# Centring the first two tiles ahead of their projections, with finer weight transfers and a shorter warm-up, in a linear-attention and gated-MLP kernel

## The chip, the cores and the metric

The kernel runs on one core of one Trainium2 chip. The metric is the device time of one execution in microseconds (us); the number quoted for a kernel is the median of its runs. The kernel before takes 193.78 us (three runs, 193.72 to 194.22). Every run also reports the mean clock that TensorE was granted (1.0 is full speed); runs with a low clock and a time over 1.5% above the fastest are called slow, and are compared with nothing here.

Engines: PE is TensorE (matmuls; PEld is its weight load), DVE is VectorE, ACT is ScalarE, POOL is GpSimd, SP is SyncE, which only issues DMA transfers. An ending q (SPq) means the engine's queue of issues.

## The reference, cut

```python
x = A_x                                                  # 2048 rows of 448, bf16
h  = x + attn(_layernorm(x), wqkv, wo)                   # linear attention, 16 heads of 28
h2 = h + (gelu(n(h) @ w_gate) * (n(h) @ w_up)) @ w_down  # n = _layernorm; 448 -> 1792 -> 448

# inside attn, with q, k, v = split(x @ wqkv):
phi = lambda t: where(t > 0, t + 1, exp(t)) + 1e-6
kv  = einsum(phi(k), v);  z = sum(phi(k))                # sums over all 2048 rows
o   = phi(q) @ kv / (phi(q) . z + 1e-6)
```

The layernorm has no learned scale. A row's `(x - mean) * rstd` can therefore be multiplied with the weights first and by `rstd` afterwards, since `rstd` is one number per row. The change uses this.

## The kernel before

The 2048 rows are 16 tiles of 128. Every operation is a task in a graph; a table `ORDERS` says in which order each of the five engines runs its tasks, and the orders have been tuned. Each engine works through its list strictly in order and waits on semaphores.

For each tile: statistics on DVE, `ln` and `rstd` on ACT (two tiny instructions, about 0.2 to 0.3 us each), then the normalised tile is transposed so that it can be projected. Tiles 0 to 3 are transposed by PE, tiles 4 to 15 by DMA.

```python
def ln_tile(t):
    ln_stats(t, ...)                       # DVE
    ln_rstd_act(t, ...)                    # ACT: Ln, then Exp(-0.5 * ln)
    if t < 4:                              # tiles 0..3
        op("dve", tensor_scalar(xnn, x_sb, mean, rstd, subtract, mult), name="normD_t")
        ...                                # 4 PE transposes of xnn; copies out of PSUM on ACT and DVE
    else:                                  # tiles 4..15
        ln_negm(t, ...)                    # POOL
        op("pool", tensor_scalar(xnn, x_sb, -mean, rstd, add, mult), name="normP_t")
        G.add("sp", dma_start_transpose(xnT[t], xnn), name="xT_t")
...
def k_tile(t):                             # K projection, 4 matmuls of 448 columns
    G.add("pe", proj(...), name="k_t")
    act_exp(activation(e1, psK, Exp), name="ek_t")
    op("dve", tensor_scalar(e1, e1, 1+EPS, 0, min, max), name="ck_t")
    op("dve", scalar_tensor_tensor(pk, psK, EPS, e1, max, add), name="pk_t")
    ...                                    # then matmuls of pk with xnn, accumulated over all tiles
def q_tile(t):                             # Q projection
    ...                                    # ACT: Exp "eq_t" and Relu "rq_t", both out of PSUM
```

(Python shortened; cuts are marked by dots.) The projections share four PSUM slots, and a slot comes free when ACT (and for K also DVE) has read it. Before the first transposes PE runs 40 dummy matmuls of 128 columns (`WARM = 40`), because its clock starts at half speed (in the profile of before they start 107 ns apart at first, and 56 ns apart once the clock has opened).

The order in which the first transfers are issued on SP: x tile 0, the Q/K weights in one piece of 672 KB and a tail of 112 KB, x tiles 2 and 3 together, 4 to 7, 8 to 11, 12 to 15, then the V and output weights. (x tile 1 is issued by ACT.)

## Time and profile before

| | before |
|---|---|
| time, median of three runs | 193.78 us |
| span of the profiled execution | 197.8 us, a slow one: clock 0.95 |
| PE busy | 193.7 us, 98% |
| share of PE in the chain that ended last | 90% |
| first projection starts | 6.31 us |

The page of the kernel before, its head, the busy times (share of the span, number of instructions), and the chain of waits by engine:

```profile
span 197.8 us, 4145 instructions
...
PE 193.7 (98%) x1572; PEld 106.9 (54%) x1572; DVE 132.0 (67%) x355; ACT 78.1 (39%) x226; POOL 50.7 (26%) x92
...
PE 90%; DMA 4%; DVE 4%; POOL 1%; issue 0%; DVEq 0%; POOLq 0%
```

PE is nearly always busy and holds nine tenths of the chain. So the reading was: what can be won is what PE does not do in its first microseconds. PE's timeline of that stretch (columns: start, duration, engine, line, operation, result and inputs, shapes, count; in brackets the idle time just before, and what ended it):

```profile
1.11 4.30 PE L342 MATMUL ps<-ones_bf 128*128 128x128 bf16 x40 [1.11 <-POOL ones_bf L315]
5.37 0.38 PE L378 MATMUL ps<-ident,xnn 128*128 128x128 bf16 x4
6.07 0.40 PE L378 MATMUL ps<-ident,xnn 128*128 128x128 bf16 x4 [0.32 <-DVE xnn L370]
6.31 3.30 PE L404 MATMUL ps<-wqk_sb,xnT 128*128 128x448 bf16 x16
```

The reader sees 40 warm-up matmuls from 1.11 us, the transposes of tile 0 at 5.37, those of tile 1 at 6.07 after a wait of 0.32 us for DVE, and then sixteen projection matmuls. Up to 6.31 us PE does, apart from these transposes, no work that counts.

### The profile page before, as it was taken

How to read it: one execution, taken by the hardware profiler on the slowest of the kernel's cores; microseconds unless marked ns; L12 is line 12 of the kernel's file. 1: busy time of each engine (PE TensorE's matmuls, PEld its weight loads, DVE VectorE, ACT ScalarE, POOL GpSimd, SP SyncE). 2: the span in 40 equal slices, each digit the busy share in tenths (PEclk: the TensorE clock that was granted, in tenths of full speed). 3: DMA queues.
4: the chain of work that ended last, by engine and by line, in shares of the span. 5: the costliest groups of instructions: out<-in, count | busy, mean ns of one | idle time of the engine just before them, and what ended most of it. 6: DMA issues, size and time to landing. Idle time of an engine off the chain costs nothing.

```text
span 197.8 us, 4145 instructions
## 1 busy us (share of the span) xinstructions
PE 193.7 (98%) x1572; PEld 106.9 (54%) x1572; DVE 132.0 (67%) x355; ACT 78.1 (39%) x226; POOL 50.7 (26%) x92
## 2 busy tenths in 40 slices
PE   7999999999999999999999999999999999999995
PEld 7554555555767776654454445444444454444454
DVE  3899988999999989988786537244445422444412
ACT  3797645599943324141330420023444200334200
POOL 7067710640451955235222024000000000000000
PEclk9999999999999999999999999999999999999999
DMA  6966449994587046420217272600200010100011
GB/s 194 375 174 88 94 96 209 221 215 63 102 291 124 16 50 117 102 53 23 56 26 153 57 56 52 133 21 30 46 0 3 0 46 4 46 0 3 0 46 46
DMA packets 35331, 16.97 MB, mean 86 GB/s; under 512 B 27696, under 2 KB 34032, under 8 KB 35312
## 3 DMA queue, kind: packets, MB, share of 16 engines
q1 hardware_dynamic: 35168, 16.60, 38.4%
q8 instruction: 12, 0.20, 0.4%
q10 hardware_dynamic: 144, 0.11, 0.2%
q14 instruction: 7, 0.06, 0.1%
HBM read 8.26 MB, written 1.84 MB: 51 GB/s over the span
## 4 chain that ended last, share of the span: by engine, by line
PE 90%; DMA 4%; DVE 4%; POOL 1%; issue 0%; DVEq 0%; POOLq 0%
PE ps L603 42%; PE ps L575 22%; PE ps L404 9%; PE ps L523 7%; PE ps L423 5%; PE ps L605 3%; DMA x_sb<-in_A_x_dram 2%; DVE st L348 2%; DMA xnT<-xnn 2%; DVE pk L417 1%; PE ps L471 0%; PE ps L462 0%; POOL wqk_sb L302 0%; PE ps L550 0%; DVE xnn L370 0%; DVE mv L349 0%
## 5 line engine op out<-in xcount | busy, mean ns | idle before, releaser
L605 PE MATMUL ps<-hnT,wgu_sb 64*128 64x512 bf16 (+1 forms) x490 | 89.9, 342 | 0.0
L603 PE MATMUL ps<-hnT,wgu_sb 64*128 64x512 bf16 (+1 forms) x490 | 89.6, 342 | 0.0
L623 ACT ACTIVATE gl<-ps 128x256 bf16<-128x256 f32 x112 | 37.1, 381 | 88.5 <-PE ps L605 86.4
L603 PEld LDWEIGHTS ps<-hnT,wgu_sb 64*128 64x128 bf16 x490 | 46.3, 96 | 35.1 <-issue 3.1
L625 DVE TENSOR_TENSOR hh<-ps,gl 128x256 bf16<-128x256 f32 x112 | 42.5, 416 | 34.0 <-ACT gl L623 33.7
L605 PEld LDWEIGHTS ps<-hnT,wgu_sb 64*128 64x128 bf16 x490 | 45.2, 96 | 3.7 <-DVE hh L625 0.5
L575 PE MATMUL ps<-wd_sb,hh 128*128 128x448 bf16 (+1 forms) x238 | 45.2, 351 | 0.0
L575 PEld LDWEIGHTS ps<-wd_sb,hh 128*128 128x128 bf16 x238 | 23.3, 99 | 21.1 <-issue 1.3
L404 PE MATMUL ps<-wqk_sb,xnT 128*128 128x448 bf16 x128 | 28.2, 362 | 0.1
L488 POOL TENSOR_TENSOR t<-pq,zbc 128x448 f32<-128x448 bf16 x15 | 16.6, 1115 | 33.3 <-DVE pq L484 20.5
L579 DVE TENSOR_TENSOR x_sb<-ps,x_sb 128x448 bf16<-128x448 f32 (+1 forms) x17 | 10.0, 592 | 19.6 <-PE ps L575 19.6
L348 DVE BATCH_NORM_STATS2 st<-x_sb 128x6 f32<-128x448 bf16 x32 | 19.1, 612 | 3.5 <-DMA x_sb<-in_A_x_dram 3.4
L404 PEld LDWEIGHTS ps<-wqk_sb,xnT 128*128 128x128 bf16 x128 | 12.3, 99 | 12.1 <-DMA xnT<-xnn 0.5
L423 PE MATMUL ps<-pk,xnn 128*128 128x448 bf16 x64 | 14.4, 363 | 0.0
L523 PE MATMUL ps<-w,pqnT 112*128 112x448 bf16 x64 | 14.1, 362 | 0.0
L558 POOL TENSOR_SCALAR hn<-x_sb,nm,rs 128x448 bf16<-128x448 bf16 x14 | 10.9, 779 | 8.1 <-DMA hnT<-hn 7.4
L529 DVE TENSOR_TENSOR x_sb<-ps,x_sb 128x448 bf16<-128x448 f32 x16 | 9.5, 617 | 3.8 <-PE ps L523 3.8
L415 ACT ACTIVATE e<-ps 128x448 bf16<-128x448 f32 x16 | 8.7, 541 | 5.4 <-PE ps L404 3.6
L417 DVE SCALAR_TENSOR_TENSOR pk<-ps,e 128x448 bf16<-128x448 f32 x16 | 9.9, 616 | 0.2
L388 POOL TENSOR_SCALAR xnn<-x_sb,nm,rs 128x448 bf16<-128x448 bf16 x12 | 9.0, 749 | 3.5 <-ACT rs L357 3.5
L423 PEld LDWEIGHTS ps<-pk,xnn 128*128 128x128 bf16 x64 | 6.5, 101 | 6.2
L495 DVE TENSOR_TENSOR pqn<-pq,rd 128x448 bf16<-128x448 bf16 x16 | 9.6, 622 | 0.0
(65 smaller groups left out, 125.0 us busy)
## 6 DMA issues: line engine op xcount, KB each, us to landing
out_dram<-x_sb SPq DMA_DIRECT2D x15, 112.0 KB, 1.7
wd_sb<-in_B_w_down_dram SPq DMA_DIRECT2D x1, 1568.0 KB, 7.7
x_sb<-in_A_x_dram SPq DMA_DIRECT2D x3, 448.0 KB, 5.4
wgu_sb<-in_B_w_gate_dram SPq DMA_DIRECT2D x1, 896.0 KB, 11.9
wgu_sb<-in_B_w_up_dram SPq DMA_DIRECT2D x1, 896.0 KB, 16.5
wqk_sb<-in_A_wqkv_dram SPq DMA_DIRECT2D x1, 672.0 KB, 4.8
wgu_sb<-in_B_w_gate_dram SPq DMA_DIRECT2D x1, 672.0 KB, 6.0
wgu_sb<-in_B_w_up_dram SPq DMA_DIRECT2D x1, 672.0 KB, 8.4
```

Of the source, the lines that this page charges most:

```text
L348: op("dve", lambda e: e.bn_stats(st[:, t, :], src_ap), [b_src], [b_st[t]], "bnst%s_%d" % (tag, t))
L404: ins = e.matmul(ps[:, bk, 0:D], xnT[:, t, k, :], wqk_sb[:, k, c0:c0 + D], start=(k == 0), stop=(k == 3))
L417: op("dve", lambda e: e.scalar_tensor_tensor(pk[:, ip, :], psK, EPS, e1[:, i, :], ALU.max, ALU.add), [b_ps[bk], b_e1[i]], [b_pk[ip]], "pk_ ...
L423: ins = e.matmul(ps[:, BK_PT[c], 0:D], xnn[:, t % XN_R, c * 128:(c + 1) * 128], pk[:, ip, :], start=(t == 0), stop=(t == T - 1))
L488: op(eng, lambda e, t=t, n=n: e.tensor_tensor(t1[:, n, :], pq[:, t, :], zbc[:, :], ALU.mult), [b_pq[t]] + b_z, [b_t1[n]], "t1%s_%d" % (eng ...
L523: ins = e.matmul(ps[:, BK_OUT[n], 0:D], pqnT[0:GW, i2, n, g, :], w2[:, g, :], start=(g == 0), stop=(g == NG - 1))
L558: op("pool", lambda e, t=t, sh=sh: e.tensor_scalar(hn[:, sh, 0:D], x_sb[:, t, :], nm2[:, t:t + 1], rs2[:, t:t + 1], ALU.add, ALU.mult), [b ...
L575: ins = e.matmul(psO, hh[:, j, (t % HR) * 128:(t % HR + 1) * 128], wd_sb[:, j, c0:c1], start=(j == 0), stop=(j == NJ - 1))
L603: e.matmul(psG[:, jj * N:(jj + 1) * N], wgu_sb[A_, k, j * 128:(j + 1) * 128], hnT[A_, ka_, c0:c0 + N], start=(k == 0), stop=(k == NK - 1))
L605: ins = e.matmul(psU[:, jj * N:(jj + 1) * N], wgu_sb[B_, k, j * 128:(j + 1) * 128], hnT[B_, kb_, c0:c0 + N], start=(k == 0), stop=(k == NK ...
L623: G.add("act", lambda e, gi=gi, cs_=cs_, psG=psG: e.activation(gl[:, gi, cs_], psG[:, cs_], AF.Gelu_apprx_tanh), r=[b_ps[BK_G[i]]], w=[b_g ...
L625: op("dve", lambda e, dst=dst, srcU=srcU, srcL=srcL: e.tensor_tensor(dst, srcU, srcL, ALU.mult), [b_ps[BK_U[i]], b_glh], [b_ar[j_][t % HR] ...
```

## The change

The intent is to start the first projection sooner and to keep it from waiting for the weights:

- Tiles 0 and 1 are only centred (`x - mean`) before they are transposed and projected. `rstd` is applied later, as the scale of the Exp and Relu with which ACT reads their projections. K's `max` on DVE becomes a Relu on ACT for these two tiles. The normalised tiles are still needed for the later matmuls with `pk`; POOL makes them.
- The Q/K weights come in four pieces, with x tile 2 between the second and the third; the following x transfers are smaller too.
- 32 warm-up matmuls in place of 40.
- The order table of every engine was computed anew.

```diff
@@ cut to its core; the order tables, all renumbered, are left out @@
+    CEN = (0, 1)
-    WARM = 40
+    WARM = 32
...
-        dma_w3("sp", wqk_sb, 0, 2 * D, b_wqk, "dwqk")
-        dma_w1("sp", wqk_sb, 0, 2 * D, b_wqk, "dwqk_t")
-        dma_x("sp", 2, 4)
-        dma_x("sp", 4, 8)
+        dma_wqk(0)
+        dma_wqk(1)
+        dma_x("sp", 2, 3)
+        dma_wqk(2)
+        dma_wqk(3)
+        dma_x("sp", 3, 4)
+        dma_x("sp", 4, 6)
+        dma_x("sp", 6, 8)
...
+                if t in CEN:
+                    op("dve", lambda e: e.tensor_scalar(xc[:, t % 2, 0:D], x_sb[:, t, :], mv1[:, t, 0:1], None, ALU.subtract), ..., "cen_%d" % t)
...
-            else:
+            if t >= N_PE_TR or t in CEN:
                 ln_negm(t, t + 1, mv1, nm1, b_mv1, b_nm1, "1")
                 op("pool", ..., "normP_%d" % t)
...
+            sc = rs1[:, t:t + 1] if t in CEN else 1.0
+            eks.append(act_exp(lambda e: e.activation(e1[:, i, :], psK, AF.Exp, scale=sc), ..., "ek_%d" % t))
+            if t in CEN:
+                act_exp(lambda e: e.activation(pk[:, ip, :], psK, AF.Relu, scale=sc), ..., "rk_%d" % t)
+                op("dve", ..tensor_scalar(e1, e1, 1.0, EPS, ALU.min, ALU.add).., "ck_%d" % t)
+                op("dve", ..tensor_tensor(pk, pk, e1, ALU.add).., "pka_%d" % t)
...
+            act_exp(lambda e: e.activation(eq[:, t, :], ps[:, bk, 0:D], AF.Exp, scale=sc), ..., "eq_%d" % t)
+            act_exp(lambda e: e.activation(pq[:, t, :], ps[:, bk, 0:D], AF.Relu, scale=sc), ..., "rq_%d" % t)
```

## The prediction

> **What bounds the kernel now.** TensorE. The busy table has PE at 193.7 of 197.8 us (98%), and the chain of waits gives it 90%. Taking single matmuls, from the first projection at 6.31 us to the end they follow at the rate of their columns (197 ns for 448 at the granted clock of 0.95), with gaps of only 2.6 us in all; the largest are 0.28 us (9.6 us, transposes of tile 3) and 0.22 us (18.1 us, a wait for a DMA transpose). The profiled execution was a slow one; the timed ones took 193.78. The change leaves the matmul work alone, so it wins only what it takes off the first 6.31 us and those gaps.
>
> **What gates 6.31 us (timeline, landings).** x tile 0 lands at 3.34; statistics to 4.21; ln and rstd on ACT to 4.77; scaled subtract to 5.22; transposes at 5.36. Tile 1's scaled subtract waits for its rstd until 5.61, its transposes run at 6.06, and PE takes them before the first projection: 6.31. The big Q/K weight piece landed at 6.03, its tail at 6.29. The 40 warm-up matmuls run 1.11 to 5.36: spaced 107 ns up to 5.03, then 56 ns.
>
> **What the change does.**
> - Removes ln+rstd (0.6 us with hand-overs) ahead of tile 0's transposes. But DVE is in order: statistics 0, centre 0, statistics 1 (0.8), half the copy of tile 0 (0.2), centre 1 (0.38), then tile 1's transposes, which still precede the first projection. Adding up from 3.37: centre 1 done near 5.85, first projection near 6.2, only 0.1 us earlier.
> - Four weight pieces: at the roughly 400 KB/us of the DMA slices they land near 4.9, 5.4, 6.2 and 6.4, x tile 2 near 5.8 instead of 6.74. Weights leave the path; tile 2's transposes move from 9.45 to about 7.9.
> - Adds two Relu evictions on ACT (0.43 us each at their spacing), a scale operand on eight activations, two normalisations on GpSimd (0.75 each). The Trainium skill ("ScalarE: Activation LUTs", What ACT_TABLE_LOAD costs) gives 93 ns for each per-partition pointer operand; before has none on these evictions, so its trace can't confirm it. ACT is busy 4.94 of 5 us from 10 to 15 us; its queue delays tile 2's copy out of PSUM: tile 2's K projection at 9.8 to 10.1, against 10.21.
> - Shorter warm-up: 32 x 107 ns ends near 4.55, before the transposes, which frees nothing. The skill ("TensorE: Matmul & The Clock Gate", Part 1) says the clock opens after a free-running activity window of about 3.4 us; the trace has it 4.0 us after the first matmul. With 3.4 us of warm-up and pauses after, it may open late in some runs: 7 projections at half clock would cost about 1.3 us, part hidden.
>
> **Sum.** First projection -0.1; transposes' gap -0.2; later gap -0.1 to -0.2; new PE waits behind ACT +0.1 to +0.2: net -0.3 us. Predicted 193.5 us, 8 in 10 within 192.5 to 194.4; faster by over 2% 0.01, within 2% 0.97, slower 0.02.
>
> **What would show it.** First projection at 6.1 to 6.3; pieces landed before their matmuls; tile 2's transposes at about 8; ACT nearly full from 6 to 16 us, evictions of tiles 0 and 1 some 90 ns longer; everything after 50 us shifted by the same few tenths.
>
> **What would make it wrong.** The clock opening late (projections spaced 373 ns at first): about 1 us slower. Tile 1's transposes not delaying the first projection, or the earlier statistics carrying through to the DMA transposes: up to 1 us faster. ACT's longer queue holding PSUM slots: up to 0.5 us slower.

## The result, and the profile after

The changed kernel is slower by 1.4%: clear of the noise. A ratio here is the mean time of one kernel's fast runs over the mean of the other's in the same rounds, so it is not quite the ratio of the medians that are quoted.

| | before | after |
|---|---|---|
| time, median (lowest to highest), six runs each | 194.05 us (193.72 to 194.8) | 197.09 us (195.81 to 197.44) |
| ratio of fast runs, 95% interval | | 1.0143, 1.0109 to 1.0176 |
| first projection starts (fast profile) | 6.75 us | 6.03 us |
| 17th projection matmul starts | 10.52 us | 12.12 us |
| span of the fast profile | 192.4 us | 195.5 us |

The profile of before that was at hand for the prediction was a slow one. So the kernel before was run once more, unchanged, for a fast profile; this is the run e0_before below, and every "before" from here on is that one. The heads of the two pages, before and then after:

```profile
span 192.4 us, 4145 instructions
...
PE 188.3 (98%) x1572; PEld 106.7 (55%) x1572; DVE 131.1 (68%) x355; ACT 77.7 (40%) x226; POOL 50.9 (26%) x92
```

```profile
span 195.5 us, 4142 instructions
...
PE 188.9 (97%) x1564; PEld 101.3 (52%) x1564; DVE 131.4 (67%) x355; ACT 78.6 (40%) x228; POOL 53.6 (27%) x97
...
PE 85%; DVE 3%; DMA 2%; ACT 0%; issue 0%; POOL 0%; DVEq 0%
```

PE works about as long as before (188.9 against 188.3 us), but the span is 3.1 us longer: the loss is time in which PE waits or runs at half clock. PE's timeline of the stretch where the two part, before and then after (some lines left out):

```profile
...
6.75 3.19 PE L404 MATMUL ps<-wqk_sb,xnT 128*128 128x448 bf16 x16
...
10.53 0.74 PE L404 MATMUL ps<-wqk_sb,xnT 128*128 128x448 bf16 x3
```

```profile
...
5.80 0.40 PE L395 MATMUL ps<-ident,xc 128*128 128x128 bf16 x4 [0.69 <-DVE xc L384]
6.03 0.54 PE L422 MATMUL ps<-wqk_sb,xnT 128*128 128x448 bf16 x2
7.19 0.36 PE L422 MATMUL ps<-wqk_sb,xnT 128*128 128x448 bf16 x1 [0.61 <-DMA wqk_sb<-in_A_wqkv_dram]
7.76 1.98 PE L422 MATMUL ps<-wqk_sb,xnT 128*128 128x448 bf16 x5 [0.21 <-DMA wqk_sb<-in_A_wqkv_dram]
9.53 0.63 PE L395 MATMUL ps<-ident,xnn 128*128 128x128 bf16 x4
...
19.49 1.69 PE L422 MATMUL ps<-wqk_sb,xnT 128*128 128x448 bf16 x8 [0.17 <-DMA xnT<-xnn]
...
26.36 0.92 PE L422 MATMUL ps<-wqk_sb,xnT 128*128 128x448 bf16 x4 [0.64 <-ACT e L435]
...
41.28 1.00 PE L489 MATMUL ps<-pt_sb,wv_sb 128*112 128x112 bf16 x16 [0.37 <-DVE pt_sb L483]
```

The first projection does start 0.72 us sooner (6.03 against 6.75; the slow profile of before had 6.31, so a part of this is chance between executions). But a projection is four matmuls, one for each weight piece: only two of them run at 6.03, and the second projection starts at 8.04 us, against 7.50 before (from the records). PE waits twice for a weight piece, 0.61 and 0.21 us; it waits at 19.49 us for a transposed tile; at 26.36 us for 0.64 us; and at 41.28 us for a copy on DVE. All the waits of PE between 5 and 50 us, before and then after (columns: who waited, for whom; us in total, times, longest):

```profile
PE ps L404 <- ACT eq L431: 0.2, 1, 0.2
```

```profile
PE ps L422 <- DMA wqk_sb<-in_A_wqkv_dram: 0.8, 2, 0.6
PE ps L395 <- DVE xc L384: 0.7, 1, 0.7
PE ps L422 <- ACT e L435: 0.6, 1, 0.6
PE ps L489 <- DVE pt_sb L483: 0.4, 1, 0.4
...
PE ps L422 <- DMA xnT<-xnn: 0.2, 1, 0.2
```

The 0.7 us for DVE's centring is the wait at 5.80 us, ahead of the first projection. Before had one wait of 0.2 us in all this time.

One of the names misleads. The 0.6 us put down to "ACT e" is the wait at 26.36 us, before the K projection of tile 10. An Exp on ACT does end just before, at 26.30 us, but it is that of K tile 9, which this projection neither reads nor overwrites. What it does read is the transposed tile 10, and that landed at 26.22 us. The view of the transposed tiles, after, says the same: who waited for their DMA (us, times):

```profile
...
  PEld ps L422: 0.8, 2
  PE ps L422: 0.2, 1
```

PE's weight load, which takes the transposed tile, waited twice for one, 0.8 us in all. So a releaser's name is a guess from times; the program's dependences decide.

There is one more loss in this execution. The granted clock and PE's busy time in two stretches of 3.41 us (columns: busy us and instructions of PE, PEld, DVE, ACT, POOL; then PE clock, DMA share, GB/s):

```profile
4.45:7.86 3.41, 1.78 (x14) 0.79 (x13) 2.16 (x8) 1.82 (x8) 0.97 (x3) 1.00 0.99 308
7.86:11.28 3.42, 3.42 (x13) 1.65 (x13) 3.32 (x10) 2.73 (x8) 1.89 (x5) 0.50 0.97 347
```

The clock had opened at 4.45 us, but in the window that followed PE was busy for only 1.78 us of 3.41, and for the next 3.41 us it was granted half. The projections there stand 373 ns apart instead of 189. The Trainium skill ("TensorE: Matmul & The Clock Gate", Part 1) describes a free-running window of about this length that both opens and closes the clock, and this trace agrees. In the kept traces with clock records the fall goes with how empty such a window is: after and e12 fell after windows with 1.78 and 1.76 us of PE work, and no trace fell after a window with 1.99 us or more. Where the windows lie is chance: in e13, with the same start, the clock opened at 5.37 us, the next window held 2.48 us, and the clock stayed. So it happens in only some executions: three of the six runs after had a mean clock of 0.99 (197.06 to 197.44 us), three had 1.0 (195.81 to 197.12). Half clock for 3.41 of 195.5 us makes a mean of 0.991, which is what the profiled run has.

How far PE had come by what time, from the matmul records of the traces (start in us of the n-th matmul of 448 columns; there are 200 or so until 50 us):

| matmul | before | after | after minus before |
|---|---|---|---|
| 1st | 6.75 | 6.03 | -0.72 |
| 17th | 10.52 | 12.12 | +1.60 |
| 41st | 15.07 | 16.89 | +1.82 |
| 81st | 22.78 | 24.80 | +2.02 |
| 121st | 30.34 | 33.16 | +2.82 |
| 161st | 38.73 | 42.11 | +3.38 |
| 200th | 47.12 | 50.47 | +3.35 |

After 50 us nothing more is lost. So the profiled execution lost 2.3 us between the first and the 17th matmul (weight pieces and half clock), 0.4 until the 81st, 0.8 until the 121st (the wait at 26.36 us) and 0.6 until the 161st (the DVE copy at 41.28 us). That reads like an explanation. The experiments show why it is not one yet: take the first loss away, and PE meets the next thing that is late.

### The profile page after: what moved, and what is told of

Its sections match the earlier page's. It is cut to its first block, busy times and chain, and to the rows that moved or that the text cites. A ratio compares the mean times of both kernels' runs of the same rounds, so it can differ in the third digit from the quotient of the medians.

```text
span 195.5 us, 4142 instructions
## 1 busy us (share of the span) xinstructions
PE 188.9 (97%) x1564; PEld 101.3 (52%) x1564; DVE 131.4 (67%) x355; ACT 78.6 (40%) x228; POOL 53.6 (27%) x97
## 4 chain that ended last, share of the span: by engine, by line
PE 85%; DVE 3%; DMA 2%; ACT 0%; issue 0%; POOL 0%; DVEq 0%
PE ps L632 23%; PE ps L602 22%; PE ps L630 22%; PE ps L422 8%; PE ps L550 7%; PE ps L448 3%; DMA xnT<-xnn 2%; DVE den L518 1%; DVE pq L511 1%; PE ps L498 0%; PE ps L577 0%; DVE t L515 0%; DVE pt_sb L478 0%; ACT e L435 0%; DVE pqn L522 0%; DVE kvm L493 0%
## 5 line engine op out<-in xcount | busy, mean ns | idle before, releaser
L632 PE MATMUL ps<-hnT,wgu_sb 64*128 64x512 bf16 (+1 forms) x490 | 87.1, 334 | 0.0
L630 PE MATMUL ps<-hnT,wgu_sb 64*128 64x512 bf16 (+1 forms) x490 | 86.5, 334 | 0.0
L632 PEld LDWEIGHTS ps<-hnT,wgu_sb 64*128 64x128 bf16 x490 | 42.5, 94 | 24.7 <-DVE hh L652 7.6
L630 PEld LDWEIGHTS ps<-hnT,wgu_sb 64*128 64x128 bf16 x490 | 43.4, 94 | 15.8 <-issue 2.2
L602 PE MATMUL ps<-wd_sb,hh 128*128 128x448 bf16 (+1 forms) x238 | 43.2, 342 | 0.0
L422 PE MATMUL ps<-wqk_sb,xnT 128*128 128x448 bf16 x128 | 29.0, 367 | 1.6 <-DMA wqk_sb<-in_A_wqkv_dram 0.8
L515 POOL TENSOR_TENSOR t<-pq,zbc 128x448 f32<-128x448 bf16 x15 | 17.5, 1170 | 29.5 <-DVE pq L511 17.9
L360 DVE BATCH_NORM_STATS2 st<-x_sb 128x6 f32<-128x448 bf16 x32 | 19.2, 612 | 4.6 <-DMA x_sb<-in_A_x_dram 4.6
L550 PE MATMUL ps<-w,pqnT 112*128 112x448 bf16 x64 | 13.6, 353 | 0.0
L448 PE MATMUL ps<-pk,xnn 128*128 128x448 bf16 x64 | 13.6, 353 | 0.0
L405 POOL TENSOR_SCALAR xnn<-x_sb,nm,rs 128x448 bf16<-128x448 bf16 x14 | 10.3, 740 | 7.8 <-ACT rs L369 6.2
L435 ACT ACTIVATE e<-ps 128x448 bf16<-128x448 f32 x14 | 7.5, 546 | 6.8 <-PE ps L422 6.8
L518 DVE TENSOR_REDUCE den<-t 128x16 f32<-128x448 f32 x16 | 9.7, 604 | 0.0
```

The source lines that it names most:

```text
L360: op("dve", lambda e: e.bn_stats(st[:, t, :], src_ap), [b_src], [b_st[t]], "bnst%s_%d" % (tag, t))
L422: ins = e.matmul(ps[:, bk, 0:D], xnT[:, t, k, :], wqk_sb[:, k, c0:c0 + D], start=(k == 0), stop=(k == 3))
L448: ins = e.matmul(ps[:, BK_PT[c], 0:D], xnn[:, t % XN_R, c * 128:(c + 1) * 128], pk[:, ip, :], start=(t == 0), stop=(t == T - 1))
L515: op(eng, lambda e, t=t, n=n: e.tensor_tensor(t1[:, n, :], pq[:, t, :], zbc[:, :], ALU.mult), [b_pq[t]] + b_z, [b_t1[n]], "t1%s_%d" % (eng ...
L518: op("dve", lambda e, n=n, i=i: e.tensor_reduce(den[:, i, :], t1[:, n, :].rearrange("p (h d) -> p h d", h=H), AX.X, ALU.add), [b_t1[n]], [ ...
L550: ins = e.matmul(ps[:, BK_OUT[n], 0:D], pqnT[0:GW, i2, n, g, :], w2[:, g, :], start=(g == 0), stop=(g == NG - 1))
```

## The experiments

Theory A, formed from this reading: the transfers and the warm-up lose the time (they starve PE early, and its clock falls back). Rival B: the centring loses it, by its extra work on ACT. Rival C: the new orders lose it, by putting small tasks that others wait for behind large ones. Below, "its before" is the kernel before, run on the same chip in the same rounds. All results were correct.

### e0_before: the kernel before, for a fast profile

```diff
  (no edit)
```

> The kernel before itself, for a profile in the fast state (the one at hand is of the slow state). About 194.1 us; no TensorE waits over 0.6 us between 10 and 45 us.

Measured: 194.08 us at clock 1.0, span 192.4. It gives the lines shown above. It also shows what had been hidden by the slow profile. From 15 to 31 us PE projects the keys of twelve tiles that were transposed by DMA, all issued by SP, one after the other. SP's queue of them, before and after (start, duration of the whole group), and the latency from issue to landing (us, least, median, most):

```profile
12.02 16.05 SPq L390 DMA_TRANSPOSE xnT<-xnn  x12
```

```profile
L390 SPq DMA_TRANSPOSE xnT<-xnn x12: 1188/1264/1547, 12.0 to 26.8; - x12
...
DMA to landing us min/median/max: 2.4/2.5/3.5
```

```profile
12.81 17.99 SPq L408 DMA_TRANSPOSE xnT<-xnn  x12
```

```profile
L408 SPq DMA_TRANSPOSE xnT<-xnn x12: 1201/1265/1647, 12.8 to 29.5; - x12
...
DMA to landing us min/median/max: 2.5/2.6/3.7
```

One issue takes 1.26 us of SP (median), so at best one transposed tile comes every 1.31 us or so (issue to issue in the records), and it lands 2.5 us after its issue. PE before used tile 6 only 0.05 us after its landing, tile 10 after 0.16, tile 8 after 0.38, the others after 0.45 to 1.29 us (from the records). The kernel before is thus bound by two things at once: PE is full, and the transposes come just in time. Whatever delays one of the first transposes delays those behind it in the queue, and PE then waits. An early start does not help against this queue. The profiles of e0, e9 and e11, kernels that take the same time, reach the 17th matmul at 10.52, 10.17 and 10.01 us, and the 121st at 30.34, 30.32 and 30.52: the half microsecond won early is gone. The prediction had called this a gap of 0.22 us.

### e1_warm40, e2_old_dma, e3_old_dma_warm40: the changed kernel, with parts undone

```diff
# e1, against after          # e2, against after            # e3: both edits
-    WARM = 32               -  the eight new transfers
+    WARM = 40               +  dma("sp", wqk_sb[:, 0:3, :], ...)   one piece
                             +  dma("sp", wqk_sb[A_, 3, :], ...)    tail
                             +  dma_x("sp", 2, 4);  dma_x("sp", 4, 8)
```

> The changed kernel (197.1 us) with 40 warm-up matmuls again, everything else as changed. Theory W (the shorter warm-up leaves the clock window too empty, and the clock falls back to half from 7.9 to 11.3 us in some runs): 195.0 to 196.0, granted clock 1.0 in all runs. Theory D (the split transfers land late and starve TensorE): no more than 0.4 us won, 196.6 to 197.1, and the half-clock stretch still there in some runs, because the first projections wait for weights either way. Theory O (the new orders and longer evictions): 196.6 to 197.1.

> The changed kernel with the transfers of before (Q/K weights in one three-block piece and a tail, x in 2-4, 4-8), warm-up 32, centring and new orders kept. Theory D: weights land by 6.3 us, the queue's last initial transfer near 12.6 instead of 15.0, time 194.8 to 195.6. Theory W: still a half-clock stretch in some runs, 196.5 to 197.1. Theory O: 196.5 to 197.1 with full clock and late landings gone.

> Transfers and warm-up both as before; only the centring and the new orders stay. If D and W together are all of it: 193.5 to 194.2, as before. Theory O (orders and longer evictions cost on their own, seen as TensorE waits of 0.8 us at 26 us and 0.5 us at 41 and 43 us): 194.8 to 196.

| | median us | its before | ratio (95%) |
|---|---|---|---|
| e1 | 196.58 | 194.11 | 1.0121 (1.0092 to 1.0149) |
| e2 | 196.71 | 194.11 | 1.0127 (1.0103 to 1.0150) |
| e3 | 196.53 | 194.11 | 1.0108 (1.0082 to 1.0134) |

Theory A fails as the main cause. With the old transfers and the old warm-up together, 2.1 us of the loss remain (1.08% of 194.1). The profile of e3 shows why. The clock stays at 1.0 and no weight piece is waited for, yet the 17th matmul starts at 11.24 us (before 10.52, after 12.12), its largest early wait being 0.8 us for DVE's normalisation of a tile. Then its transposes are issued from 12.51 to 29.59 us (17.08 us in place of 16.05 before), PE waits 0.6 us at 25.4 us, where the transpose of tile 10 landed at 25.29, and 0.4 us for the same DVE copy as after.

### e4_before_new_dma, e10_before_weights_split, e11_before_x_split: the transfers alone

```diff
# e4, against before: all transfers of after
# e10, against before: only the weights in pieces
-        dma_w3("sp", wqk_sb, 0, 2 * D, b_wqk, "dwqk")
-        dma_w1("sp", wqk_sb, 0, 2 * D, b_wqk, "dwqk_t")
+        dma_wqk(0); dma_wqk(1); dma_wqk(2); dma_wqk(3)
# e11, against before: only the finer x
-        dma_x("sp", 2, 4);  dma_x("sp", 4, 8)
+        dma_x("sp", 2, 3);  dma_x("sp", 3, 4);  dma_x("sp", 4, 6);  dma_x("sp", 6, 8)
```

> The kernel before with nothing but the split transfers. Theory D: slower by 1 to 2 us (195.0 to 196.0), pieces of the weights landing up to 7.7 us and the last initial transfer near 15. Theories W and O: 193.6 to 194.4, as before.

> The kernel before with the Q/K weights alone in four pieces, x as before. If it is the cutting of the weights that lets the DMA engines drift apart: second piece landing spread over more than 1 us, last initial transfer near 15 us, slower by about 0.8 us as with both. If it is the finer x: spread under 0.9 us, last near 12.7, time within 0.2 us of before.

> The kernel before with x alone cut finer (2, 3, 4-5, 6-7). If the finer x makes the engines drift apart: last initial transfer near 15 us and slower by 0.5 to 0.9 us. If the weights do: last near 12.7 to 13, within 0.2 us of before.

| | median us | its before | ratio (95%) |
|---|---|---|---|
| e4 | 194.89 | 194.11 | 1.0035 (1.0020 to 1.0050) |
| e10 | 195.45 | 194.43 | 1.0047 (1.0018 to 1.0075) |
| e11 | 194.19 | 194.43 | 0.9985 (0.9957 to 1.0012) |

The pieces cost 0.7 to 0.9 us in a kernel that is otherwise the one before; the finer x costs nothing. What moved in 5 to 10 us, for before, after and e10 (columns as in the windows above):

```profile
5.00:10.00 5.00, 4.84 (x34) 2.74 (x31) 4.33 (x14) 3.37 (x12) 0.00 (x0) 1.00 1.04 382
```

```profile
5.00:10.00 5.00, 3.48 (x19) 1.64 (x18) 3.71 (x12) 2.92 (x9) 2.21 (x5) 0.79 0.96 318
```

```profile
5.00:10.00 5.00, 4.74 (x33) 2.50 (x31) 3.61 (x11) 3.06 (x11) 0.00 (x0) 1.00 1.00 339
```

The last number is the traffic: 382 GB/s before, 318 after, 339 with only the pieces. A transfer is shared out over 16 DMA engines (the records hold sixteen landings for each) and has landed when the last has. From the records, the one large piece before landed on all engines between 5.04 and 5.53 us. The second piece landed between 4.18 and 6.00 us after, and between 4.23 and 5.68 in e10. Over all kept traces the large piece takes 0.4 to 1.0 us from the first engine to the last (1.4 in e7), the second of four pieces 1.2 to 1.9 us. Most engines are early and a few are more than a microsecond late, and the late ones stay late for the next transfers: the last of the first transfers (the output weights) lands at 12.69 us before, 15.01 after, 15.19 in e4, 14.40 in e10. The Trainium skill says that nothing orders DMAs across the 16 engines ("DMA: Bandwidth & Descriptors", Two DMAs through the same engine are not ordered); that agrees. Why small pieces let them drift further was not found. In the end PE's largest wait is at the familiar place: in e10 0.6 us at 19.2 us for a DMA transpose, in e4 0.7 us at 15.9 us. But e11, which costs nothing, shows such a wait of 0.7 us too, so one wait in one profile is not the cost; that the pieces cost time through the transposes is likely, not shown.

### e7_before_warm32: the shorter warm-up alone

```diff
-    WARM = 40
+    WARM = 32
```

> The kernel before with 32 warm-up matmuls. If the shorter warm-up costs by itself (clock opens later or falls back): 194.5 to 195.5 with a granted clock under 1.0 in some runs. If not: within 0.3 us of before, 193.8 to 194.4.

Measured: 195.79 us against 194.2; ratio 1.0068 (1.0023 to 1.0113). Single runs: 195.7, 196.25, 195.88, 194.26. The profiled one shows the first sixteen projection matmuls (four projections):

```profile
6.62 4.67 PE L374 MATMUL ps<-wqk_sb,xnT 128*128 128x448 bf16 x16
```

They take 4.67 us; before they took 3.19 (line 6.75 above). In this execution the clock opened only at 9.64 us. So the shorter warm-up costs about 1.7 us in three runs of four (1.5 to 2.1) and nothing in the fourth. That fits a window that runs freely of the kernel's start, but only the one profiled run shows the clock. In the changed kernel going back to 40 (e1) wins only some 0.4 us, which is within the intervals.

### e5_centre_old_orders and e6_new_orders_no_centre: the centring and the orders, each alone

```diff
# e5, against after: WARM = 40, the transfers of before, and ORDERS = those of before,
#     with the new tasks put in beside the ones they replace
# e6, against before: CEN = (), ORDERS = those of after less the tasks of the centring;
#     ln and rstd of tile 1 had to be moved forward, else the engines wait for each other
```

> Centring alone: transfers, warm-up and the orders of before, with the new operations put in beside those they belong to. If the orders cost the time: 193.7 to 194.6. If the centring itself does (longer evictions on ACT, two more of them): 195.5 to 196.6, as with the new orders (196.5).

> The new orders alone: no centring, transfers and warm-up of before. If the orders cost the time: 195.5 to 196.6, with the waits of TensorE near 25, 40 and 42 us (0.8, 0.5, 0.5 us). If the centring does: 193.8 to 194.6.

| | median us | its before | ratio (95%) |
|---|---|---|---|
| e5 | 196.32 | 194.2 | 1.0117 (1.0091 to 1.0142) |
| e6 | 197.40 | 194.2 | 1.0170 (1.0142 to 1.0198) |

Both cost, so neither B nor C falls here. But e6 is not a clean measure of the orders: without the centring, these orders make PE wait 1.3 us for DVE's normalisation of a tile and 1.4 us for `pk`, waits that the changed kernel does not have. The sum of the parts by their ratios is 0.7 (e4) + 1.3 (e7) + 2.3 (e5) + 3.3 (e6) = 7.6 us, against 2.8 by the ratio of after. The parts do not add. The likely reason is that each delays PE before the same slots and transposes, and the largest delay covers the others; no run shows this by itself.

### e8_before_act_load and e9_before_scale_operand: only the work that the centring puts on ACT

```diff
# e9, against before: a column of ones as scale for the evictions of tiles 0 and 1
+            sc = one_s[:, 0:1] if t < 2 else 1.0
-  activation(e1, psK, AF.Exp)
+  activation(e1, psK, AF.Exp, scale=sc)               # the same for eq and rq
# e8: e9, and a useless pass where the centring has its Relu
+            if t < 2:
+                act_exp(activation(dm[:, t, :], x_sb[:, t, :], AF.Relu, scale=sc), ..., "rk_%d" % t)
```

> The kernel before with only ACT's extra work of the change, all of it useless: two Relu passes of tiles 0 and 1 into a scratch tile and a scale column of ones on the six evictions of tiles 0 and 1. Theory A (ACT is the limit from 7.7 to 17 us, and the extra work of about 0.52 us a Relu and 0.1 us a scale operand shifts everything behind it): slower by 1.2 to 1.7 us, 195.3 to 195.8. Rival (the centring costs by its other parts, on DVE, GpSimd or in the order of readiness): within 0.3 us of before.

> The kernel before with the scale column of ones alone on six evictions. Theory A: each of the six about 95 ns longer, 0.57 us on ACT, slower by 0.3 to 0.6 us. Rival: no change beyond 0.2 us.

e9: 194.31 us against 194.43, ratio 0.9993 (0.9966 to 1.0019). e8: 195.57 us, ratio 1.0048 (1.0016 to 1.0080). The scale operands alone cost nothing, the two passes with them about 0.9 us. (The pass reads SBUF, and takes about as long: 664 ns, against 630 for the Relu of after.) The operand's own price can be read in one kernel. The Exp of K tiles in after from 8 to 17 us, with and without the scale `rs` (count; busy us, mean ns):

```profile
L435 ACT ACTIVATE e<-ps,rs 128x448 bf16<-128x448 f32 x2 | 1.2, 620 | 0.0
...
L435 ACT ACTIVATE e<-ps 128x448 bf16<-128x448 f32 x2 | 1.1, 548 | 0.0
```

620 against 548 ns; in e9 the Exp evictions of tiles 0 and 1 take 0.61 to 0.64 us where before took 0.52 to 0.54. The Trainium skill gives 93 ns for each such operand ("ScalarE: Activation LUTs", What ACT_TABLE_LOAD costs), and this agrees. e8 reproduces the profiled execution of e5 closely: the 17th matmul starts at 10.81 us (e5 10.86, before 10.52), the span is 194.0 (e5 193.9). By medians e5 loses 2.1 us and e8 1.1, so about 1 us of e5's loss is not covered by ACT's load, and no profile of a slower run of e5 exists to show it.

### e12_after_rstd_first and e13_after_rstd_first_evp2: the changed kernel with two orders mended

What the traces of the orders had shown: DMA transposes wait for POOL's normalisation, which waits for `rstd` from ACT. POOL's lines from 10 to 18 us, before and then after (L388 and L405 are the normalisations of tiles 4, 5, ...):

```profile
...
11.28 0.71 POOL L388 TENSOR_SCALAR xnn<-x_sb,nm,rs 128x448 bf16<-128x448 bf16 x1 [0.82 <-ACT rs L357]
...
12.69 0.71 POOL L388 TENSOR_SCALAR xnn<-x_sb,nm,rs 128x448 bf16<-128x448 bf16 x1 [0.52 <-ACT rs L357]
```

```profile
...
12.06 0.72 POOL L405 TENSOR_SCALAR xnn<-x_sb,nm,rs 128x448 bf16<-128x448 bf16 x1 [1.19 <-issue]
15.01 0.72 POOL L405 TENSOR_SCALAR xnn<-x_sb,nm,rs 128x448 bf16<-128x448 bf16 x1 [2.23 <-ACT rs L369]
```

Tile 5 is normalised at 12.69 us before and at 15.01 after, where POOL sat idle for 2.23 us until ACT wrote `rs`. ACT's lines in that time, before and then after:

```profile
...
12.36 0.23 ACT L357 ACTIVATE rs<-ln 128x1 f32<-128x1 f32 x1
```

```profile
...
13.90 0.29 ACT L367 ACTIVATE ln<-mv,eps_t 128x1 f32<-128x1 f32 x1
14.09 0.54 ACT L459 ACTIVATE pq<-ps 128x448 bf16<-128x448 f32 x1
14.51 0.30 ACT L367 ACTIVATE ln<-mv,eps_t 128x1 f32<-128x1 f32 x1
14.70 0.21 ACT L369 ACTIVATE rs<-ln 128x1 f32<-128x1 f32 x1
```

The line at 12.36 us is `rstd` of tile 5 before. After, its `ln` runs at 13.90 us, but then come the Relu of Q tile 2 (0.54 us) and the `ln` of tile 6, and only at 14.70 us the `rstd` of tile 5. The Trainium skill has the queues of ACT, DVE and POOL as strictly first in, first out ("TensorE: Matmul & The Clock Gate", the table at its head); the trace agrees, a 0.2 us task waits behind whatever stands before it. The transpose of tile 5 is issued at 15.75 us after, 13.43 before.

And on DVE, after and then e13, around the copy that `kv` waits for (L483 and L453, "pt_sb"):

```profile
...
38.21 1.23 DVE L511 TENSOR_TENSOR pq<-pq,eq 128x448 bf16<-128x448 bf16 x1
...
40.52 0.56 DVE L483 CAST pt_sb<-ps 128x448 bf16<-128x448 f32 x1
```

```profile
...
37.76 0.57 DVE L453 CAST pt_sb<-ps 128x448 bf16<-128x448 f32 x1
38.25 0.47 DVE L481 TENSOR_TENSOR pq<-pq,eq 128x448 bf16<-128x448 bf16 x1
```

After, an addition for Q tile 5, which nobody needs soon, stands ahead of the copy and takes 1.23 us. Where POOL does nothing it takes 0.36 to 0.39 us (244 additions in the kept traces). It ran beside POOL's product (37.72 to 39.20 us), and the Trainium skill says that DVE instructions with two SBUF inputs contend with POOL for SBUF ("GPSIMD Engine Reference", Specifications). The kept traces agree: in all eight where the addition started while this product was under way, it ended 0.24 or 0.25 us after the product, and so took 0.47 to 1.23 us.

```diff
# e12, ACT's order (names in place of numbers):
-  ek_1 rk_1 evxA_3 ek_2 ln_5 rq_2 ln_6 rstd_5 eq_2 ek_3 rq_1 rstd_6 ln_7 ln_8 rstd_7 rstd_8
+  ln_5 rstd_5 ek_1 rk_1 evxA_3 ek_2 ln_6 rstd_6 rq_2 eq_2 ek_3 ln_7 rstd_7 rq_1 ln_8 rstd_8
# e13: e12, and DVE's order:
-  aq_5 dr_0 rd_0 evpD_2
+  dr_0 rd_0 evpD_2 aq_5
```

> The changed kernel with one thing moved: on ACT the ln and rstd of tiles 5, 6, 7 and 8 stand ahead of evictions instead of behind them. Theory T (the queue of DMA transposes paces the stage, and the new order starts it late): the second transpose issued near 14.2 us instead of 15.75, the fifth near 18.8 instead of 20.2, time 195.4 to 196.1 (from 197.1). Rival (TensorE waits elsewhere, for PSUM slots behind ACT, or the clock alone): 196.7 to 197.3, although the transposes come earlier.

> The same, with one more move on DVE: the addition for tile 5's queries stands behind the copy that the kv product waits for. If that order makes the 0.53 us wait of TensorE at 41 us: wait gone or under 0.15, another 0.3 to 0.5 us won, 195.0 to 195.7. If not: as the run before.

| | median us | its before | ratio (95%) |
|---|---|---|---|
| after | 197.09 | 194.05 | 1.0143 (1.0109 to 1.0176) |
| e12 | 195.91 | 194.25 | 1.0085 (1.0046 to 1.0125) |
| e13 | 194.98 | 194.25 | 1.0034 (1.0003 to 1.0066) |

Nothing but the places of tasks was changed, with the transfers and the warm-up of after, and some 2 us of the 3 are gone. By the ratios it is 1.1 us for the first move and 1.0 for the second, but neighbouring intervals overlap; only those of after and e13 do not. The traces say what the second move is worth: from the 121st to the 161st matmul PE takes 8.94 or 8.95 us in all six fast traces with the DVE order of after (after, e1, e2, e3, e6, e12), and 8.39 to 8.41 in the twelve without it, so 0.54 us. In e13 POOL starts the normalisations of tiles 4 and 5 in one go:

```profile
...
11.16 1.46 POOL L375 TENSOR_SCALAR xnn<-x_sb,nm,rs 128x448 bf16<-128x448 bf16 x2 [0.84 <-POOL nm L334]
```

and PE no longer waits for the copy at 40 us. All four runs of e13 had clock 1.0, while three of six after had 0.99. The mean of all runs of after less the mean of its three at clock 1.0 is 0.36 us. If e13 was only lucky with the clock, that much of the difference is not the orders'; that leaves 1.7 to 2.1 us. A second pair has clock 1.0 in every run, and the same warm-up and weight transfers: e3 (1.0108) and e16 below (1.0036; its finer x cost nothing in e11). It gives 1.4 us. So the two moves are worth 1.4 to 2.1 us.

### e14_before_rstd5_late and e15_before_rstd_first: the same place in the kernel before

```diff
# e14, against before, ACT's order:
-  ln_5 ek_2 rstd_5 eq_2 rq_2 ln_6 rstd_6
+  ln_5 ek_2 eq_2 rq_2 ln_6 rstd_5 rstd_6
# e15, against before: the finer x of e11, and ln/rstd of tiles 4 and 5 ahead of the evictions on ACT
```

> The kernel before with the misplacement alone: the rstd of tile 5 put behind the ln of tile 6 on ACT, as in the new orders. Theory T: the second transpose issued about 1 us later (14.4 instead of 13.43), everything behind it too, slower by 0.6 to 1.2 us: 194.8 to 195.6. Rival: no change, 194.0 to 194.5.

> A try at a better kernel: before with the finer x transfers (which cost nothing) and the ln/rstd of tiles 4 and 5 moved ahead of evictions on ACT. First transpose issued near 11.3 us. Theory T: 0 to 0.6 us won (193.6 to 194.2), as TensorE's waits in this stage are only about 0.7 us; rival: no change or slightly slower.

e14 moves one 0.2 us task. Its fast runs took 195.74, 197.43 and 197.52 us, the last two at clock 0.991; its before took 194.25; ratio 1.013 (1.0074 to 1.0185). So the place of this one task costs 1.5 us at clock 1.0, by the one run that had it. Why the other two had a lower clock, with 40 warm-up matmuls and the old transfers, no profile shows; so neither a shorter warm-up nor pieces are needed for it. Its fourth run, the profiled one, took 247.19 us at clock 0.759, a state that no other run showed, and only the order of events is read from it: POOL waits 1.83 us for `rs` before the normalisation of tile 5, and the transpose is issued at 15.58 us, nearly as after (15.75). This is the direct test of rival C's mechanism, in a kernel without any centring.

e15 tries the other direction: 194.43 us, ratio 1.0002 (0.9974 to 1.0031). With an earlier `rstd` the kernel before gains nothing; PE there had only one wait of 0.2 us to lose.

### e16_centre_mended and e17_centre_rstd_first: what is left for the centring

```diff
# e16, against after: the orders of e13, WARM = 40, Q/K weights in one piece and a tail (finer x kept)
# e17, against e5, ACT's order:
-  ln_3 ek_0 rk_0 rstd_3 eq_0 evxA_2 ln_4 ek_1 rk_1 rstd_4 evxA_3 rq_1 ln_5 ek_2 rstd_5
+  ln_3 rstd_3 ek_0 eq_0 evxA_2 ln_4 rstd_4 rk_0 ek_1 evxA_3 ln_5 rstd_5 rk_1 rq_1 ek_2
#     and on DVE the statistics of tiles 5 and 6 and a copy of tile 3 ahead of pka_0 and ck_1
```

> The changed kernel with everything mended that the runs found: ln/rstd first on ACT, the DVE move, weights in one piece and a tail, x in finer pieces, 40 warm-up matmuls; the centring stays. If the centring's idea is worth what was hoped (first projection 0.1 to 0.6 us earlier): 193.4 to 194.1. If its ACT work eats that: 194.3 to 195.2.

> Centring with the orders, transfers and warm-up of before, but on ACT the rstd of tiles 3, 4 and 5 and the copies of tiles 2 and 3 ahead of the Relu passes, and DVE's adds behind the statistics. If the ACT work costs through the start of the transposes: first transpose issued near 12.2 us instead of 13.15 and time 194.4 to 195.3 (from 196.3). If by another path: 195.8 to 196.6.

e16, in five rounds: 195.01 us against 194.04, ratio 1.0036 (0.9997 to 1.0075). It equals e13, so once the orders are mended, and at clock 1.0, the old transfers and the old warm-up win nothing more. What remains is about 0.7 us, with an interval that just touches zero. It fits the centring's load on ACT (0.9 us in e8), but e16 also keeps the centring's work on DVE and POOL and the rest of the new orders, and no run separates these. e17: 195.76 us, ratio 1.0075 (1.0031 to 1.0119), better than e5 but not good. Its first transpose is issued at 11.44 us, earlier than before (12.02). But PE now waits elsewhere:

```profile
...
14.64 0.93 PE L388 MATMUL ps<-wqk_sb,xnT 128*128 128x448 bf16 x4 [0.90 <-ACT pq L425]
```

It waits 0.90 us for the PSUM slot of Q tile 2, which ACT's Relu finished reading at 14.58 us. This time the name is right: the Q projection of tile 3 writes that slot. ACT is busy 4.85 of the 5 us from 10 to 15 us before the change, so the extra passes leave little choice (this is a reading, not a test): they delay either the small `rstd` tasks, and with them the transposes, or the evictions, and with them the slots. No version that was run beats the kernel before.

## Why the prediction was wrong, point by point

The prediction was 193.5 us, 192.5 to 194.4; measured 197.09. "Within 2%" held, the direction and the range did not.

- "First projection near 6.2": 6.03 after. Right for its first two matmuls; its last two waited for their weights, and the second projection started later than before (8.04 against 7.50). Time won at the start is worth nothing if PE waits later.
- "Weights leave the path", with pieces landing "near 4.9, 5.4, 6.2 and 6.4" and x tile 2 "near 5.8": mis-sized. They landed at 3.99, 6.00, 7.14 and 7.71, x tile 2 at 6.33. The estimate let all pieces flow at the rate of the large one, about 400 KB/us. With pieces the traffic fell to 318 GB/s and each piece waited for its latest engine. PE waited 0.61 + 0.21 us for them, the transposes of tile 2 came at 9.53 instead of "about 7.9", and its K projection (the 17th matmul) at 12.12 instead of "9.8 to 10.1".
- "It may open late in some runs ... about 1.3 us": the mechanism was right, its chance was not. It was put among the things that would make the prediction wrong. The profiled run of e7 lost 1.5 us to it over the first sixteen projection matmuls, and three of its four runs were slow by about as much; in after, three of six runs had clock 0.99, and in the profiled one of these the clock had opened in time and fell back.
- "Evictions of tiles 0 and 1 some 90 ns longer", and two Relu passes: right (620 against 548 ns; e9 shows that the operands alone are free).
- "New PE waits behind ACT +0.1 to +0.2": mis-sized. e8 loses about 0.9 us to this load, e17 shows one wait of 0.90 us, and e16, with the other parts undone or mended, keeps about 0.7.
- "Later gap -0.1 to -0.2": this is the step that failed outright. The prediction saw one wait of 0.22 us for a DMA transpose and took it for a small gap that an earlier start would close. It is the visible end of a queue of twelve transposes that come 1.31 us apart and land 0.05 to 1.3 us before PE needs them. The gap did not shrink; PE waited 0.17 us at 19.49 and 0.64 at 26.36 us, and e14 shows that the place of one `rstd` in ACT's order can move the whole kernel by 1.5 us (one run at clock 1.0); e12, which moves `ln` and `rstd` of tiles 5 to 8, wins 1.1.
- Left out altogether: the sum had no term for the new orders. They were in the diff, and one could have read off that ACT's list has the Relu of Q tile 2 and `ln` of tile 6 between `ln` and `rstd` of tile 5, and that DVE's has an addition for tile 5 ahead of the copy for `kv`. These two placements are 1.4 to 2.1 of the 3 us.

In short, of about 3 us: 1.4 to 2.1 for the two placements, some 0.7 for what is left with them mended (ACT's extra work, most likely), the rest within the clock's lottery and the intervals. The pieces and the warm-up cost 0.7 to 1.3 us when they stand alone, but in the changed kernel undoing both wins only about 0.6 (within the intervals), and with mended orders nothing.

What stays open: why pieces let the DMA engines drift; about 1 us by which e5 loses more than e8; and why in each profile one transpose or more takes about a microsecond longer than the others (up to 3.5 us before, for tile 6, and 3.7 after, for tile 5, in place of 2.5). In the traces looked at, an instruction fetch of 16 KB runs about when the first of these is under way, and one of 8 KB during the transpose of tile 10 (after, at 24.11 us; this transpose took 3.4 us, and PE then waited at 26.36), but that was only seen, not tested.

## What to carry to other kernels

When an engine is 98% busy, look at how early its inputs arrive, not only at where it waits: before, the transposed tiles landed as little as 0.05 us ahead of their use, so 2 us of delay of one `rstd` could not be absorbed. When a change comes with a new order for the engines, read the orders like code: find each small task that a chain of other engines hangs on (`rstd`, a copy that a matmul waits for) and see what stands before it. And when parts of a change are tested alone, expect their costs not to add; undo them in the changed kernel as well, and mend one suspect at a time.

## What the Trainium skill lacked or had wrong

- "DMA: Bandwidth & Descriptors": its latency table gives 261 GB/s for the effective bandwidth of a DMA transpose (one kernel, with a non-contiguous middle dimension). No page gives the pace at which queued transposes of 128 x 512 follow each other within SBUF. Here SP needs 1.26 us to issue one (median of twelve), they follow each other every 1.31 us, and each lands 2.5 us after its issue (at most 3.7 in before and after). A tile of 128 x 512 in bf16 is 131 KB, so that is 100 GB/s; the pace is nearly that of SP's issues, so this does not contradict the page's figure.
- The same page says that DMAs are not ordered across the 16 engines, but not how far a transfer's parts drift: 0.4 to 1.0 us from first to last for one piece of 672 KB (1.4 in one trace of fourteen), 1.2 to 1.9 us for the second of four pieces. Traffic between 5 and 10 us was 382 GB/s before and 318 after.
- "TensorE: Matmul & The Clock Gate", Part 1, table of the two states: the clock falls back "after ≥1 idle window". Here a window need not be idle. Counting windows of 3.41 us from the opening in the kept traces with clock records, the clock fell after windows with 1.78 us (after), 1.76 (e12) and, at the end of the program, 1.0 (e9) and 0.98 us (e7) of PE work, and after none with more; the least that kept it open was 1.99 us (e6). The same part puts the ramp's penalty at less than 1% of a typical span, and that agrees; but with this kernel, of 194 us, a warm-up eight matmuls shorter costs about 1.7 us (0.9%) in three runs of four and nothing in the fourth, which is over half of what the whole change lost.
